# Part of the K phases on GpSimd, products by channel half, resident swapped spectra, and the last reads in two row groups

## The chip, the cores and the metric

One core of one Trainium2 chip. The metric is the device time of one execution in microseconds (us). "Time" below is a median over executions; the "span" of a profile runs from the first to the last instruction of the one execution that was profiled, and is about 2 us shorter than its time. Engine names are those of the profile: PE (TensorE), PEld (its weight loads), DVE (VectorE), ACT (ScalarE), POOL (GpSimd), SP (the queue that issues transfers). All runs compared here are in the fast state; single slower executions were left out by the comparison itself.

## The reference

One layer that mixes a long convolution with a gated feed-forward network, over 2048 tokens of 640 channels:

```python
g = sigmoid((x * gate_w).sum(-1, keepdims=True))
a = irfft(rfft(pad(u)) * rfft(pad(K)))[:L] + u * Dskip   # K[d,l] = Re sum_n C*dB*exp(dt*A*l)
b = (gelu(x @ w_gate) * (x @ w_up)) @ w_down
out = g * a + (1 - g) * b                                # x = u
```

## The kernel before

The kernel is one list of steps (some 900), each with a function and the buffers it reads and writes. A constant, `ORDER`, fixes the order of emission and the engine and PSUM bank of each step. So every change of the algorithm comes with a new order of all engines.

The kernel K of the convolution is made in two channel halves. For each half, "phases" (integer angles) are computed, ACT takes their sine, DVE combines the tables, and PE contracts them. These are the phases, all on DVE before:

```python
def phases(q, grid, i0):
    ...
    def go():
        for j in range(4):
            i, o = i0 + j, ph[:, 1, :, 4 * j:4 * j + 4]                  # 128x320
            if grid == 1:
                nc.vector.tensor_scalar(out=o, in0=quads(bK[:, ds]), scalar1=float(4 + 8 * i), ..., op0=ALU.mult)
            else:
                nc.vector.scalar_tensor_tensor(out=o, in0=quads(bK[:, ds]), ..., in1=quads(phiK[:, ds]), ...)
        nc.vector.tensor_scalar(out=ph[:, 0], in0=ph[:, 1], scalar1=PH / 4, ..., op0=ALU.add)   # 128x1280
```

The transforms go through memory: dU and dKA (spectra half-way), dY (the result before the last transform). For each of eight chunks c, `mix` loads dKA, finishes the K spectrum, multiplies it on DVE with the spectrum U and with its copy Us whose row pairs are swapped, and transforms back:

```python
def mix(u, us, kb, bi, c, UK, keys, R):
    ks = stageB(loadB(dKA[:], keys, bi, c, R), t, tn, R)
    ve(..., tensor_tensor(out=U,  in0=U,  in1=t, op=ALU.mult))     # 128x2560
    ve(..., tensor_tensor(out=Us, in0=Us, in1=t, op=ALU.mult))
    ...                                # inverse on PE, copies to t, write of t to dY chunk c
def finish(keys, rings, R):            # rings: four buffers
    for g in range(8):
        dma(640, ... out=t, in_=dY[:, 4 * g:4 * g + 4, :] ...)     # needs all dY chunks
        ...                            # two products on PE, DVE adds into the output, two output writes
```

## Time and profile before

| what | value |
|---|---|
| time | 329.29 us median of 3 (326.54 to 329.34) |
| profiled execution | 327.61 us, span 325.8 us |
| first / second K contraction starts on PE | 100.4 / 182.3 us |
| last forward matmul of K / last inverse starts | 238.4 / 295.7 us |

The prediction shows the lines that carry its argument. Four more matter later. From the groups of instructions (line, engine, operation, output and inputs, count, then busy time, mean ns of one, idle time before it) come the two-input products on DVE, whose means are the yardstick for any disturbance. From the list of transfers (count, KB each, median us from issue to landing) comes the dY round trip.

```profile
L637 DVE TENSOR_TENSOR arena<-arena 128x2560 bf16<-128x2560 bf16 x10 | 14.7, 1482 | 0.0
L631 DVE TENSOR_TENSOR arena<-arena 128x1280 bf16<-128x1280 bf16 x10 | 7.9, 816 | 1.0 <-ACT arena L627 1.0
...
dY<-arena SPq DMA_DIRECT2D x8, 640.0 KB, 6.1
arena<-dY SPq DMA_DIRECT2D x8, 640.0 KB, 5.6
```

### The profile page before, as it was taken

The numbers are of one execution on the slowest core, as the hardware profiler recorded it, in microseconds if no ns is written. First come the engines' busy times: TensorE is split into PE (matmuls) and PEld (weight loads), VectorE is DVE, ScalarE is ACT, GpSimd is POOL, SyncE is SP. The second block draws the span as 40 slices with busy tenths as digits, with TensorE's granted clock in tenths as the row PEclk, the third lists the DMA queues.
The fourth block names the chain that finished last, engine by engine and source line by source line (L and its number), as shares of the span: only waits on it lengthen the run. The fifth ranks groups of instructions, "written<-read, shape, count | busy, mean of one in ns | idle before, by whom it ended". The sixth has DMA issues, their size and how long they took to land.

```text
span 325.8 us, 5490 instructions
## 1 busy us (share of the span) xinstructions
PE 266.1 (82%) x2112; PEld 146.7 (45%) x2126; DVE 246.3 (76%) x332; ACT 223.6 (69%) x307; POOL 5.3 (2%) x18
## 2 busy tenths in 40 slices
PE   0799999897796999979899987985998889993452
PEld 0254444443366677534344743432465456551220
DVE  4687999999999963799996977254363899982464
ACT  4998997699995599998989576525471386671000
POOL 3000000000000000000000000000110000000000
PEclk9989999999797999999999997999899799998555
DMA  6993344332321144433437659979366569934997
GB/s 171 394 331 104 121 140 125 100 103 81 125 76 42 62 123 130 143 123 120 141 100 240 188 192 291 341 163 260 115 204 221 181 240 330 344 141 163 368 353 245
DMA packets 47519, 60.57 MB, mean 186 GB/s; under 512 B 4419, under 2 KB 41862, under 8 KB 47494
## 3 DMA queue, kind: packets, MB, share of 16 engines
q1 hardware_dynamic: 47494, 60.23, 57.3%
q8 instruction: 16, 0.26, 0.3%
q14 instruction: 9, 0.07, 0.1%
HBM read 35.80 MB, written 19.17 MB: 169 GB/s over the span
## 4 chain that ended last, share of the span: by engine, by line
PE 36%; ACT 22%; DVE 18%; DMA 15%; issue 5%; SPq 3%; DVEq 0%; ACTq 0%
PE ps L548 13%; PE ps L520 8%; PE ps L500 7%; ACT arena L243 6%; ACT arena L589 5%; DVE arena L247 5%; DMA dKA<-arena 4%; ACT arena L599 4%; DMA arena<-dY 3%; DMA arena<-dU 3%; ACT arena L504 3%; DMA arena<-dKA 2%; DVE arena L859 2%; PE ps L650 2%; PE ps L807 2%
## 5 line engine op out<-in xcount | busy, mean ns | idle before, releaser
L243 ACT CAST arena<-ps 128x640 bf16<-128x640 f32 x111 | 70.6, 702 | 38.1 <-PE ps L807 15.7
L500 PE MATMUL ps<-arena 128*128 128x512 bf16 x276 | 66.5, 392 | 13.0 <-DMA arena<-in_u_T_dram 9.2
L247 DVE CAST arena<-ps 128x640 bf16<-128x640 f32 (+2 forms) x67 | 56.2, 881 | 20.1 <-PE ps L807 10.4
L520 PE MATMUL ps<-arena 128*128 128x512 bf16 x250 | 63.1, 401 | 4.2 <-DVE arena L524 1.9
L548 PE MATMUL ps<-arena 128*128 128x320 bf16 x448 | 65.0, 305 | 1.0 <-DVE arena L247 0.5
L548 PEld LDWEIGHTS <-arena 128*128 128x128 bf16 x448 | 44.5, 100 | 20.6 <-issue 2.1
L500 PEld LDWEIGHTS <-arena 128*128 128x128 bf16 x280 | 28.0, 100 | 47.9 <-issue 14.1
L520 PEld LDWEIGHTS <-arena 128*128 128x128 bf16 x260 | 26.5, 103 | 37.2 <-issue 9.3
L589 ACT ACTIVATE arena<-arena 128x2560 bf16<-128x2560 int16 x18 | 41.6, 2334 | 0.4 <-DVE arena L637 0.3
L524 DVE TENSOR_TENSOR arena<-ps,arena 128x1024 bf16<-128x1024 f32 x26 | 31.6, 1218 | 13.1 <-PE ps L520 12.9
L504 ACT ACTIVATE arena<-ps 128x1024 bf16<-128x1024 f32 (+1 forms) x28 | 27.7, 1023 | 9.4 <-PE ps L500 9.2
L807 PE MATMUL ps<-arena 64*64 64x320 bf16 x256 | 16.9, 325 | 9.0 <-DMA arena<-dKA 2.8
L599 ACT ACTIVATE arena<-arena 128x320 bf16<-128x320 f32 x64 | 23.3, 455 | 1.0 <-DVE arena L451 1.0
L854 PE MATMUL ps<-arena 128*64 128x320 bf16 x64 | 10.2, 474 | 14.5 <-DMA arena<-dY 14.5
L859 DVE SCALAR_TENSOR_TENSOR arena<-ps,g_f,arena 128x640 bf16<-128x640 f32 x16 | 13.0, 878 | 11.9 <-PE ps L854 11.9
L249 DVE TENSOR_SCALAR arena<-ps,omg 128x640 bf16<-128x640 f32 x10 | 8.8, 883 | 14.9 <-PE ps L548 14.9
L627 ACT ACTIVATE arena<-arena 128x320 bf16<-128x320 f32 x40 | 14.8, 455 | 5.9 <-PE ps L650 5.9
L582 DVE SCALAR_TENSOR_TENSOR arena<-arena 128x320 int32<-128x320 f32 x40 | 16.9, 483 | 0.8 <-ACT arena L589 0.7
L650 PE MATMUL ps<-arena 128*128 128x80 bf16 x320 | 13.5, 212 | 3.8 <-DVE arena L637 2.8
L807 PEld LDWEIGHTS <-arena 64*64 64x64 bf16 x256 | 8.2, 107 | 17.7 <-issue 9.7
L650 PEld LDWEIGHTS <-arena 128*128 128x128 bf16 x320 | 13.3, 107 | 4.6 <-DVE arena L637 3.5
L780 PE MATMUL ps<-arena 128*128 128x320 bf16 x64 | 12.1, 308 | 4.1 <-DMA arena<-dS 2.3
(93 smaller groups left out, 240.8 us busy)
## 6 DMA issues: line engine op xcount, KB each, us to landing
arena<-in_w_gu_dram SPq DMA_DIRECT2D x52, 160.0 KB, 2.2
dU<-arena SPq DMA_DIRECT2D x16, 320.0 KB, 2.3
arena<-dU SPq DMA_DIRECT2D x8, 640.0 KB, 4.7
dKA<-arena SPq DMA_DIRECT2D x16, 320.0 KB, 4.2
arena<-arena SPq DMA_DIRECT2D x16, 320.0 KB, 4.3
arena<-dKA SPq DMA_DIRECT2D x8, 640.0 KB, 6.0
dY<-arena SPq DMA_DIRECT2D x8, 640.0 KB, 6.1
arena<-dY SPq DMA_DIRECT2D x8, 640.0 KB, 5.6
```

Source lines behind the costliest of these rows:

```text
L243: nc.scalar.copy(out=dst, in_=src(b))
L247: nc.vector.tensor_copy(out=dst, in_=src(b))
L500: nc.tensor.matmul(ps[:, k + j, :], lhsT=Wg[w][:, kt, :], rhs=xT[2 * grp + j][:, kt, :], start=(kt == 0), stop=(kt == NKT - 1))
L504: add({"ACT": an(1024)}, lambda s: nc.scalar.activation(out=HTall[0:p, :, f, :], in_=ps[0:p, plan.bank(g):plan.bank(g) + 2, :], func=ACT.G ...
L520: nc.tensor.matmul(ps[:, k + j, :], lhsT=Wu[w][:, kt, :], rhs=xT[2 * grp + j][:, kt, :], start=(kt == 0), stop=(kt == NKT - 1))
L524: add({"DVE": v1(1024)}, lambda s: nc.vector.tensor_tensor(out=HTall[:, :, f, :], in0=ps[:, plan.bank(u):plan.bank(u) + 2, :], in1=HTall[: ...
L548: nc.tensor.matmul(ps[:, k + h, 0:W], lhsT=HTq[q][:, f, 128 * j:128 * j + 128], rhs=Wd[f][:, W * h:W * h + W], start=(f == 0), stop=(f == ...
L589: ac(an(8 * W), lambda: nc.scalar.activation(out=t[:], in_=ph.bitcast(I16)[:, :, :, 0:32:2], func=ACT.Sin, scale=SIN_SCALE), r=[f"ph{k}"], ...
L599: nc.scalar.activation(out=cs1[:, 1, :, 4 * s:4 * s + 4], in_=quads(aT[:, ds]), func=ACT.Exp, scale=float(sg * (4 + 8 * i)))
L650: nc.tensor.matmul(ps[:, k + i // g, 80 * (i % g):80 * (i % g) + 80], lhsT=cs1[:, x, k0 + i, :], rhs=cs2[:, x, k0 + i, :], start=(x == 0), ...
L807: nc.tensor.matmul(ps[64 * y:64 * y + 64, k + x, 0:W], lhsT=TB[64 * x:64 * x + 64, 0, :], rhs=t[64 * x:64 * x + 64, 2 * a + y, HV[h]], sta ...
L859: add({"DVE": v1(D)}, lambda s, p=p, ph=ph, z=z: nc.vector.scalar_tensor_tensor(out=z, in0=ps[:, plan.bank(p):plan.bank(p) + 2, 0:W], scal ...
```

## The change

Its intent: take work from DVE in the first two stages (GpSimd was idle), begin spectral products when half of the channels are there, take the swap transfers out of the late stage, and read a part of dY before all of it is written.

```diff
-        def go():
+        def ts(s, **kw):
+            (nc.gpsimd if s["eng"] == "POOL" else nc.vector).tensor_scalar(**kw)
+        def go(s):
...
-        ve(4 * (v2(W) if grid == 1 else v1(W)) + v2(4 * W), go, ...)
+        e1 = {"DVE": 4 * (v2(W) if grid == 1 else v1(W))}
+        if grid == 1:
+            e1["POOL"] = 4 * pn(W)
+        add(e1, go, ...)
+        add({"DVE": v2(4 * W), "POOL": pn(4 * W)}, lambda s: ts(s, out=ph[:, 0], in0=ph[:, 1], ... op0=ALU.add), ...)
...
-    dKA = dp.tile([128, 32, D], BF16, name="dKA")
+    dKA = [dp.tile([128, 32, W], BF16, name=f"dKA{h}") for h in range(2)]
...
-    def mix(u, us, kb, bi, c, UK, keys, R):
+    def product(h, u, us, kb, bi, c, UK, keys, R):        # one channel half: U, Us times t, 128x1280 each
+    def inverse(u, us, yb, c, UK, R):
...
-    Us = blocks(O_CS1 + 40960, 4, 5120, 4, "Vs")
+    Us = (... eight buffers: every swapped spectrum stays ...)
...
+        for q in range(2):
+            p0, p1 = (0, 16 * cut) if q == 0 else (16 * cut, 128)       # cut = 4: rows 0-63, 64-127
+            for g, (t, nm) in enumerate(tiles):
+                dma(..., out=t[p0:p1], in_=dY[p0:p1, 4 * g:4 * g + 4, :], r=[("dY", c) for c in range(p0 // 16, p1 // 16)])
...
-    finish(ys, blocks(O_CS1, 4, 5120, 4, "as"), P["F1"])
+    finish(blocks(O_CS1, 4, 5120, 4, "as") + blocks(O_CS1 + 40960, 4, 5120, 4, "at"), P["F1"], 4)
```

`ORDER` is replaced as a whole. In it GpSimd gets 14 phase steps: 16 multiplications of 128x320 and 10 additions of 128x1280.

## The prediction

> **What bounds the kernel now.** I read the page's busy table first, then the row of 40 slices, then the windows (one table by stage), then the chain that ended last in order of time, and last the timeline of the final stage.
>
> ```profile
> PE 266.1 (82%) x2112; PEld 146.7 (45%) x2126; DVE 246.3 (76%) x332; ACT 223.6 (69%) x307; POOL 5.3 (2%) x18
> PE   0799999897796999979899987985998889993452
> DVE  4687999999999963799996977254363899982464
> POOL 3000000000000000000000000000110000000000
> ```
>
> No engine is full over the whole run, but each stage has its own limit: DVE (with ACT) to about 100 us, PE after that, nobody after 297. POOL does nothing. The windows say it in numbers (columns: window, length, busy of PE, PEld, DVE, ACT, POOL, granted clock, DMA share, GB/s):
>
> ```profile
> 40.00:80.00 40.00, 37.05 (x174) 17.12 (x176) 38.85 (x45) 35.57 (x46) 0.00 (x0) 1.00 0.38 111
> 80.00:120.00 40.00, 34.05 (x333) 23.78 (x334) 37.59 (x53) 32.34 (x49) 0.00 (x0) 0.87 0.25 78
> 275.00:290.00 15.00, 13.61 (x190) 8.83 (x192) 14.51 (x14) 9.45 (x16) 0.00 (x0) 1.00 0.77 268
> 300.00:310.00 10.00, 4.42 (x30) 2.04 (x32) 4.46 (x6) 0.00 (x0) 0.00 (x0) 0.50 0.84 318
> ```
>
> The end of the chain shows the tail. Read it as: the last down projection (L548) and the last inverse transform, then a round trip through memory, then a DVE-paced finish that twice waits for a read.
>
> ```profile
> 290.55 3.98 PE ps L548 x28
> ...
> 297.05 3.20 DMA dY<-arena
> 300.30 0.35 issue
> 300.74 3.89 DMA arena<-dY
> 304.67 0.76 PE ps L854 x3
> 305.54 1.53 DVE arena L859 x2
> 307.13 4.85 DVE arena L859 x6
> 311.98 0.31 SPq L863
> 312.38 7.01 DMA arena<-dY
> 319.43 0.76 PE ps L854 x4
> ```
>
> In the timeline of that stage the first five tiles reach L854 every 1.58 us (304.67, 306.25, ...), the last three at 313.65, 317.04 and 319.43: their buffers are reused, so their reads were issued late, behind output writes. The group rows I price with:
>
> ```profile
> L859 DVE SCALAR_TENSOR_TENSOR arena<-ps,g_f,arena 128x640 bf16<-128x640 f32 x16 | 13.0, 878 | 11.9 <-PE ps L854 11.9
> L826 DVE TENSOR_TENSOR arena<-arena 128x2560 bf16<-128x2560 bf16 x8 | 11.8, 1484 | 0.4 <-ACT arena L243 0.4
> L584 DVE TENSOR_SCALAR arena<-arena 128x1280 int32<-128x1280 int32 x18 | 14.9, 827 | 0.6
> dU<-arena SPq DMA_DIRECT2D x16, 320.0 KB, 2.3
> arena<-arena SPq DMA_DIRECT2D x16, 320.0 KB, 4.3
> ```
>
> **What the Trainium skill says.** First, "SBUF — State Buffer", section "Who interferes with whom": GpSimd and VectorE share one pair of ports under an exclusive lock, held for a whole instruction; VectorE needs it for tensor_scalar in a two-port mode and for two SBUF inputs (there against a GpSimd instruction that reads SBUF), while an instruction that reads PSUM and at most one SBUF input does not contend. The kernel before has no GpSimd instruction that reads SBUF, so its trace can't tell. Second, "GPSIMD Engine Reference", section "Engine selection": elementwise work is about twice as slow there for two inputs, roughly line rate for one. The moved instructions have one input; the nearest thing in this trace is an iota of 128x1024 at 1046 ns, against 827 ns for L584's 128x1280 on DVE. Third, "SBUF — State Buffer", section "Door 1: The DMA port swizzle": partitions 0 to 63 reach only 8 of 16 ports. The trace agrees: 320 KB on 64 partitions took 4.3 us, 320 KB on 128 took 2.3 us. Fourth, "VectorE: DVE Perf Modes", on the TRN2 errata: a fixed cost per instruction, about 150 cycles. It agrees: a bf16 product of 128x1280 (L613) has a mean of 819 ns, one of 128x2560 1484 ns, so two halves cost 154 ns more.
>
> **The change part by part.**
>
> (1) GpSimd. In the built order GpSimd gets 4 of the 8 groups of four grid-1 phases (128x320) and 10 of the 18 adds of 128x1280. DVE sheds 16 x 0.26 + 10 x 0.83 = 12.4 us; 8 of the short instructions and 6 of the adds, 7.0 us, belong to the first K half. On GpSimd I estimate 0.5 and 1.4 us each from the iota's slope, so 16 x 0.5 + 10 x 1.4 = 22 us. By the lock, part of that comes back as DVE waiting; DVE reads PSUM in about a quarter of the stage to the first contraction (12 of L524 at 1.22 and 7 evacuations at 0.8: 20 of 85 us) and idles in some more, so at best half of the saving is kept.
>
> (2) Products by half. 16 products of 1.48 become 32 of 0.82: 26.2 instead of 23.7, so DVE pays 2.5 us. In return half 0 (its reads of the K spectrum, 64 of the L807 matmuls, half the products) no longer waits for half 1. The writes of the K spectrum also get rows of 1280 instead of 640 bytes.
>
> (3) Resident swapped spectra. Eight swap transfers (320 KB, 4.3 us each) leave the stage after 245 us, where the DMA share is 0.77, for the stage before. No engine's work changes.
>
> (4) Last reads in two row groups, eight separate buffers: rows 0 to 63 are read while the last chunks are computed; after the last dY write only 8 x 320 KB are left, all issued at once. They reach half the ports, so I keep 1.58 us a tile and no bandwidth gain; the gain is that tiles six to eight no longer arrive late: 1.1 + 1.7 + 0.7 = 3.5 us of DVE waiting from the timeline. The floor of the finish is 16 x 0.84 = 13.4 us on DVE.
>
> (5) A new order on every engine. This is the largest part. I priced the built order of PE with the durations before (ten matmuls of L500 or L520 2.16, 28 of L548 3.95, four of L719 0.55, of L780 0.72, of L807 0.33, 24 of L650 1.03, 16 of L834 0.72). PE work ahead of four points: the first K contraction, the second, the last K forward matmul (L780), the last inverse (L834).
> Before: 73.5, 149.6, 197.3, 250.7 us. They happened at 100.4, 182.3, 238.5 and 296.0.
> After: 63.9, 137.7, 200.2, 246.8 us.
>
> Stage 1, to the first contraction. PE does not pace it. Summing the durations before over the built orders, ACT has 89.9 us up to its last needed Sin, as before (90.1, reached at 98.1). DVE has 85.2 instead of 92.9, plus GpSimd's lock. ACT starts about half a microsecond sooner (its parameters are the first transfers) and loses its 2.5 us wait for the reciprocal, which now comes early. I put the contraction at 98, 2.4 earlier. PE gets there with 9.6 us less work done, which is a debt.
> Stage 2, to the second contraction: PE 73.8, DVE 69, ACT 71 (before 76.2, 72, 74 in 81.9). All three are as tight as before, so I scale: 79.4 us, so 177.5.
> Stage 3, to the last L780: PE 62.5 instead of 47.7. The extra work is filler where PE waited before: 56.2 us elapsed for 47.7. I expect 4 us of idle, 66.5, so 244.
> Stage 4, to the last L834: PE 46.6 instead of 53.4, because less of the transforms is left and one down projection (3.95) now comes after it. Before, 57.5 us elapsed, 4 above the sum; I take 50, so 294.
> Tail: evacuation, dY write and read 8.65 (296.0 to 304.67), first matmuls 0.87, DVE 13.4, last output 3.9 (321.9 to 325.8): 26.8. Span about 321. The moved down projection fits into the 8.65.
>
> The sum is a span 5 us shorter (1.5%). The ledger: tail 3, down projection 4, filler in stage 3 some 4 to 5, contraction 2.4, against 9.6 us of debt and a little DVE.
>
> **The rivals.** (a) GpSimd gives more than I kept: the lock is mostly taken beside PSUM work and stage 1 ends at 95; then stage 2 is looser too and the span is 312 to 316. For it: DVE at 97% of 40 to 80. Against: ACT is at 89% and has the same sum. (b) GpSimd's lock turns against DVE: each 1.4 us add stalls a DVE that would have needed 0.83; stage 1 ends at 103, and the time is 327 to 331. For it: three quarters of DVE's work in stage 1 reads and writes SBUF alone. (c) DMA becomes the bound: the swaps pile up with the gathers of half 1 (windows 200 to 215 already show a share of 0.96), and the early row-group reads sit ahead of the last dY writes, which also have only two buffers. That would cost 3 to 8 us and eat the tail's gain. Against: dY chunks come 5.4 us apart on PE (1.44 + 3.95), slow enough for the queue to drain.
>
> **Range and chances.** The stage sum gives 321 of span. Times run 1.8 (the profiled run, 327.61) to 3.5 us (the median) above it: 324. A new order that prepares filler work for each known wait is more often underrated than overrated by such a sum, since I scaled each stage by the old inefficiency; so I move the centre to 320, 2.8% under 329.3. Rivals b and c make the upper edge 328, rival a the lower 311. The 2% line is 322.7, close to the centre: faster 0.62, within 0.34, slower 0.04.
>
> **What would show it.** Right: the first contraction at 95 to 100; PE idle of at most 5 us between the second contraction and the last L780; L854's matmuls every 1.7 us without gaps and under 28 us from the last inverse to the end; the last L548 inside the dY round trip; GpSimd busy about 22 us. Wrong: the mean of DVE's SBUF products above 819 and 1484 ns beside GpSimd (rival b); late landings of dY writes or of K gathers (rival c); a first contraction before 94 (rival a).

## The result, and the profile after

The kernel after takes 343.69 us (median of four, 338.89 to 344.64; the slowest counts as slow and is left out of the ratio, a fifth execution of 341.48 is in it), the kernel before 329.06 us over the same rounds. Ratio 1.0409, 95% interval 1.031 to 1.0509: slower. A ratio here is the mean time of the one kernel's fast runs over that of the other's fast runs of the same rounds, so not quite the ratio of the medians. The profiled execution took 338.89 us (span 337.1); it is the fastest of them, so the table below understates the loss a little.

The same four points, and the end, as predicted and as seen:

| stage ends with | before | predicted | after | duration predicted | duration after |
|---|---|---|---|---|---|
| first K contraction starts | 100.4 | 98 | 106.7 | 98 | 106.7 |
| second K contraction starts | 182.3 | 177.5 | 183.5 | 79.4 | 76.8 |
| last forward matmul of K | 238.4 | 244 | 254.7 | 66.5 | 71.2 |
| last inverse starts | 295.7 | 294 | 304.3 | 50 | 49.6 |
| end of span | 325.8 | 320.8 | 337.1 | 26.8 | 32.8 |

The miss is in three stages: 8.7 us in the first, 4.7 in the third, 6.0 in the last; the second gives 2.6 back.

Next come the page's busy line and the slices of DVE and POOL. The sum of work that the order gives DVE has gone down, but its busy time has gone up by 15 us, and POOL's phase steps take 56.1 us where 22 were estimated (two lines below):

```profile
PE 266.6 (79%) x2110; PEld 145.0 (43%) x2126; DVE 261.0 (77%) x327; ACT 223.9 (66%) x304; POOL 61.4 (18%) x44
...
DVE  4978999999999979999887914433997799732564
...
POOL 4900640534675404040000000000001100000000
```

Below are the groups of POOL and of DVE, different shapes kept apart. POOL's addition takes 3.56 us and its multiplication 1.28 in the mean; on DVE, in the run without GpSimd phases, the same steps take 0.82 (mean) and 0.25 (busy time by count). POOL's means include time in which it was itself held beside DVE: its shortest addition took 3.44 us, its shortest multiplication 1.01. The DVE products of 128x1280 and 128x2560 of the K chain have means of 1020 and 1776 ns where they had 816 and 1482, and DVE's own additions 1240 where they had 827:

```profile
L582 POOL TENSOR_SCALAR arena<-arena 128x1280 int32<-128x1280 int32 x10 | 35.6, 3557 | 59.5 <-DVE arena L590 41.9 <-DVE arena L582 16.5 <-ACT arena L638 0.9
L582 POOL TENSOR_SCALAR arena<-arena 128x320 int32<-128x320 f32 x16 | 20.5, 1283 | 29.8 <-ACT arena L600 24.9 <-DVE arena L458 4.1
```

```profile
L648 DVE TENSOR_TENSOR arena<-arena 128x2560 bf16<-128x2560 bf16 x10 | 17.7, 1776 | 1.4 <-ACT arena L600 1.4
...
L642 DVE TENSOR_TENSOR arena<-arena 128x1280 bf16<-128x1280 bf16 x10 | 10.0, 1020 | 0.0
L582 DVE TENSOR_SCALAR arena<-arena 128x1280 int32<-128x1280 int32 x8 | 9.9, 1240 | 0.3
```

The timeline shows how. First DVE from 60 to 71 us, then POOL in the same time (start, length):

```profile
60.30 6.10 DVE L590 SCALAR_TENSOR_TENSOR arena<-arena 128x320 int32<-128x320 f32 x8
66.32 0.81 DVE L642 TENSOR_TENSOR arena<-arena 128x1280 bf16<-128x1280 bf16 x1
67.06 0.81 DVE L252 CAST arena<-ps 128x640 bf16<-128x640 f32 x1
67.79 2.87 DVE L642 TENSOR_TENSOR arena<-arena 128x1280 bf16<-128x1280 bf16 x1
70.59 0.81 DVE L252 CAST arena<-ps 128x640 bf16<-128x640 f32 x1
```

```profile
62.08 3.62 POOL L582 TENSOR_SCALAR arena<-arena 128x1280 int32<-128x1280 int32 x1 [15.95 <-DVE arena L590]
66.56 3.88 POOL L582 TENSOR_SCALAR arena<-arena 128x1280 int32<-128x1280 int32 x1 [0.85 <-ACT arena L638]
```

Read the second addition: it ends at 66.56 + 3.88 = 70.44. The copy from PSUM that starts inside it (67.06) takes its usual 0.81 us. The product that follows (67.79), two inputs in SBUF, ends at 70.66, just after POOL is done. The eight instructions at 60.30 take 6.10 us around the first addition; in the run without GpSimd phases (a1 below) they take 3.31. Even an instruction of 32 columns took 3.42 us at 14.08 (0.30 in a1), until POOL's run that began at 8.00 ended 9.46 us later. The kernel after, then a1:

```profile
14.08 3.42 DVE L406 TENSOR_SCALAR arena<-arena,sc 128x32 int32<-128x32 int32 x1
8.00 9.46 POOL L582 TENSOR_SCALAR arena<-arena 128x320 int32<-128x320 f32 x5 [4.10 <-DVE arena L458]
```

```profile
58.16 3.31 DVE L591 SCALAR_TENSOR_TENSOR arena<-arena 128x320 int32<-128x320 f32 x8
14.44 0.30 DVE L407 TENSOR_SCALAR arena<-arena,sc 128x32 int32<-128x32 int32 x1
```

Taken one by one in the trace, seven DVE instructions of the kernel after took 1.8 to 3.2 us longer than the shortest of their kind, 17.7 us together, each beside one of the ten additions. No DVE instruction that reads PSUM was stretched by more than 0.1 us.

The last stage has a second trouble. In the queue's timeline, seven reads of rows 0 to 63 (L861) are issued before the sixth of the eight dY writes (L854, at 295.58). That write takes 10.75 us to land, where the slowest recorded one of the kernel before took 7.6. The results on their way to dY have two buffers, and ACT waits 7.1 us for one; in the kernel before no engine waited for a dY write from 270 us on:

```profile
291.15 4.31 SPq L861 DMA_DIRECT2D arena<-dY  x7
295.58 0.52 SPq L854 DMA_DIRECT2D dY<-arena  x1
...
300.16 8.27 SPq L854 DMA_DIRECT2D dY<-arena  x2
```

```profile
ACT arena L248 <- DMA dY<-arena: 7.1, 1, 7.1
```

### The profile page after: what moved, and what is told of

It is laid out like the page before. It is cut to its first block, busy times and chain, and to the rows that moved or that the text cites. A ratio compares the mean times of both kernels' runs of the same rounds, so it can differ in the third digit from the quotient of the medians.

```text
span 337.1 us, 5542 instructions
## 1 busy us (share of the span) xinstructions
PE 266.6 (79%) x2110; PEld 145.0 (43%) x2126; DVE 261.0 (77%) x327; ACT 223.9 (66%) x304; POOL 61.4 (18%) x44
## 3 DMA queue, kind: packets, MB, share of 16 engines
q1 hardware_dynamic: 45702, 60.23, 59.2%
## 4 chain that ended last, share of the span: by engine, by line
DVE 31%; PE 21%; ACT 19%; DMA 16%; issue 7%; SPq 4%; POOLq 0%; DVEq 0%; ACTq 0%
PE ps L525 7%; PE ps L505 6%; ACT arena L248 5%; ACT arena L600 4%; DMA dY<-arena 4%; DVE arena L252 4%; PE ps L553 4%; DVE arena L529 3%; DMA arena<-dY 3%; DVE arena L590 3%; DVE arena L648 3%; ACT arena L509 3%; DVE arena L624 2%; ACT arena L610 2%; DVE arena L465 2%
## 5 line engine op out<-in xcount | busy, mean ns | idle before, releaser
L505 PE MATMUL ps<-arena 128*128 128x512 bf16 x271 | 69.8, 409 | 21.4 <-DMA arena<-in_w_gu_dram 14.5
L525 PE MATMUL ps<-arena 128*128 128x512 bf16 x253 | 65.1, 405 | 12.4 <-ACT arena L509 4.5
L252 DVE CAST arena<-ps 128x640 bf16<-128x640 f32 (+2 forms) x71 | 59.8, 876 | 16.4 <-PE ps L817 10.9
L582 POOL TENSOR_SCALAR arena<-arena 128x320 int32<-128x320 f32 (+1 forms) x26 | 56.1, 2158 | 89.3 <-DVE arena L590 41.9
L553 PE MATMUL ps<-arena 128*128 128x320 bf16 x448 | 64.7, 304 | 2.7 <-ACT arena L248 2.6
L505 PEld LDWEIGHTS <-arena 128*128 128x128 bf16 x280 | 28.8, 104 | 59.1 <-issue 17.8
L553 PEld LDWEIGHTS <-arena 128*128 128x128 bf16 x448 | 44.0, 99 | 22.1 <-issue 4.2
L525 PEld LDWEIGHTS <-arena 128*128 128x128 bf16 x260 | 26.2, 102 | 46.3 <-issue 19.9
L610 ACT ACTIVATE arena<-arena 128x320 bf16<-128x320 f32 x64 | 23.4, 454 | 1.5 <-DVE arena L456 1.5
L590 DVE SCALAR_TENSOR_TENSOR arena<-arena 128x320 int32<-128x320 f32 x40 | 22.6, 626 | 1.7 <-ACT arena L600 1.7
L897 POOL IOTA arena<- 128x1024 int32 x2 | 2.1, 1044 | 116.3 <-DMA dKA<-arena 104.4
L648 DVE TENSOR_TENSOR arena<-arena 128x2560 bf16<-128x2560 bf16 x10 | 17.7, 1776 | 1.4 <-ACT arena L600 1.4
L582 DVE TENSOR_SCALAR arena<-arena 128x320 int32<-128x320 f32 (+1 forms) x24 | 14.5, 648 | 2.3 <-ACT arena L600 2.0
```

The source lines that it names most:

```text
L252: nc.vector.tensor_copy(out=dst, in_=src(b))
L505: nc.tensor.matmul(ps[:, k + j, :], lhsT=Wg[w][:, kt, :], rhs=xT[2 * grp + j][:, kt, :], start=(kt == 0), stop=(kt == NKT - 1))
L525: nc.tensor.matmul(ps[:, k + j, :], lhsT=Wu[w][:, kt, :], rhs=xT[2 * grp + j][:, kt, :], start=(kt == 0), stop=(kt == NKT - 1))
L553: nc.tensor.matmul(ps[:, k + h, 0:W], lhsT=HTq[q][:, f, 128 * j:128 * j + 128], rhs=Wd[f][:, W * h:W * h + W], start=(f == 0), stop=(f == ...
L582: (nc.gpsimd if s["eng"] == "POOL" else nc.vector).tensor_scalar(**kw)
L610: nc.scalar.activation(out=cs1[:, 1, :, 4 * s:4 * s + 4], in_=quads(aT[:, ds]), func=ACT.Exp, scale=float(sg * (4 + 8 * i)))
```

## The experiments

Theory at the start: GpSimd's operations are far slower than estimated and hold DVE up (first stage), and the early reads delay the dY writes (last stage). Rival: the new order, with its late first matmul (14.5 us against 7.45) or its halves, costs it. Each chip has its own level, so runs of different rows are compared by their ratio to the kernel before.

| run | what it is | time | ratio to before, 95% interval |
|---|---|---|---|
| a1_no_gpsimd | after, phases back on DVE | 330.55 | 1.0060 (1.0033 to 1.0087) |
| a2_whole_reads | after, whole late reads | 341.09 | 1.0395 (1.0365 to 1.0426) |
| a3_both | both edits | 328.42 | 0.9995 (0.9964 to 1.0025) |
| b1_gpsimd_alone | before, 14 phase steps on GpSimd | 337.49 | 1.0295 (1.0257 to 1.0332) |
| b2_eight_reads | before, 8 read buffers | 326.07 | 0.9895 (0.9839 to 0.9951) |
| b3_down_last | before, last projection moved | 325.85 | 0.9880 (0.9797 to 0.9962) |
| b4_both_tail | before, b2 and b3 | 324.73 | 0.9933 (0.9907 to 0.9959) |
| c1_weights_first | a3, other first transfers | 328.02 | 0.9983 (0.9953 to 1.0014) |
| d1_reads_in_order | a3, two reads exchanged | 326.62 | 1.0010 (0.9976 to 1.0044) |
| d2_early_tokens | d1, TensorE's first inputs first | 329.41 | 1.0073 (1.0047 to 1.0100) |
| e1_idle_gpsimd | a1 with idle GpSimd work (spoilt) | 342.00 | 1.0452 (1.0369 to 1.0534) |
| e2_idle_long | a1 with idle GpSimd work | 356.74 | 1.0862 (1.0804 to 1.0919) |
| g1_short_only | after, only the multiplications on GpSimd | 335.17 | 1.0235 (1.0170 to 1.0299) |
| g2_long_only | after, only the additions on GpSimd | 340.50 | 1.0382 (1.0319 to 1.0445) |
| f1_gpsimd_fp32 | after, GpSimd in fp32 | 341.63 (one run) | state unknown |

All give the right result except f1, which is wrong on purpose.

### Taking the two suspects away

a1 changes 14 entries of the order from POOL to DVE, at the same places. a2 replaces the two row groups by one whole read per tile:

```diff
-        for q in range(2):
-            p0, p1 = (0, 16 * cut) if q == 0 else (16 * cut, 128)
...
+        for g, (t, nm) in enumerate(tiles):
+            dma(640, ... out=t, in_=dY[:, 4 * g:4 * g + 4, :], r=[("dY", c) for c in range(8)], w=[nm])
```

> The kernel after, with its fourteen phase steps (16 multiplications of 128x320, 10 additions of 128x1280) put back from GpSimd on VectorE, at the same places in the order. Theory (slow GpSimd work holds VectorE up): the first K contraction comes back from 106.7 to 98-101 us, no 3 us copies of 32 columns are left on VectorE, time 333-337 against 343.7 of the kernel after. Rival (the new order of the first stage, above all the later first matmul at 14.5 us, costs it): first contraction stays above 104, time 341-346, as VectorE then has some 12 us more of its own work.

> The kernel after, with the eight last reads whole (128 partitions each), issued after the last write of dY, all ahead of the outputs as before. Theory (the early reads of row group 0 lie ahead of the last dY writes and hold the two dY buffers): the dY write issued at 295.6 lands in 3-5 us instead of 10.75, VectorE and ScalarE lose their waits of 2.4 and 7.0 us for it, and the time falls by 3-5 us to 339-341. Rival (the reads are not what the tail waits for): within 1.5 us of 343.7; or slower by up to 3, if the early halves did save reading time.

> Both edits at once: no GpSimd phases and whole late reads. What is left of the change: products by halves, resident swaps, eight read buffers, the new order. Theory: the two losses add, 328-332, about the kernel before (329.1). Rival (order, halves or the pile of transfers in the third stage cost the rest): 334-340.

Measured: a1 gives back 3.5% (1.0409 to 1.0060), more than was expected; a2 almost nothing by itself, but on top of a1 the same edit gives 0.65% (1.0060 to 0.9995). a2's mechanism was as expected: ACT's and DVE's waits for dY writes (7.1 and 2.4 us) are gone (the sixth write's landing is missing from a2's trace, so the 3 to 5 us expected for it stay unchecked). From the last inverse to the end it takes 30.7 us instead of 32.8. That this hardly shows in its time is within the scatter of the kernel after, whose fast runs differ among themselves by 1.4%.

| point | predicted | a1 | a3 |
|---|---|---|---|
| first contraction | 98 | 98.3 | 98.1 |
| second contraction | 177.5 | 173.4 | 173.7 |
| last forward matmul of K | 244 | 244.6 | 244.3 |
| last inverse | 294 | 294.6 | 295.7 |
| end | 320.8 | 327.1 | 325.8 |

Without GpSimd four of the five points come out within 4.1 us of the prediction, three of them within 2 us in both runs. A part of that is luck: in a1 the second stage took 75.1 us where 79.4 were predicted, and the third 71.2 where it was 66.5, so that two errors of over 4 us cancel at 244.6. What stays is the end: 32.5 us from the last inverse in a1, 30.1 in a3, against 26.8 predicted.

### GpSimd alone, in the old order

b1 splits the phase step of the kernel before in two, as the change does, and gives GpSimd the same number of steps:

```diff
-    ve(4 * (...) + v2(4 * W), go, ...)                  # one step on VectorE
+    add(e1, go, ...); add({"DVE": ..., "POOL": ...}, lambda s: ts(s, out=ph[:, 0], ...))
 ORDER: each phase step becomes two at the same place; 4 and 10 of them on GpSimd
```

> The kernel before, with the same number of phase steps of the same groups on GpSimd (16 multiplications of 128x320 and 10 additions of 128x1280), nothing else changed. Theory: a multiplication takes 1.28 us and an addition 3.4-3.6 us there, VectorE's instructions beside them stretch, and the time rises by 5-12 us to 334-341. Rival (GpSimd work is harmless by itself, only the new order makes it costly): 326-331.

Measured: 1.0295, so GpSimd costs some 9 us without anything else of the change (in the change itself it is 3.5%, by a1). DVE's busy time is 255.9 us where it was 246.3 (9.6 more), the span 335.0 where it was 325.8 (9.2 more). The rival is out: the new order is not needed for this loss.

### Held port or late results

GpSimd can cost time in two ways: DVE is stretched beside it, or something waits for its results. In e1 and e2 DVE does all phases and GpSimd does work that nobody reads; g1 and g2 split the change's own GpSimd work by length. e1 has idle multiplications of 128x320, three of them for each addition. The edit of e2 (of a1; the multiplications likewise):

```diff
+        def idle2(s):
+            if s["i"] in GP:                       # the steps that GpSimd had
+                nc.gpsimd.tensor_scalar(out=scr2, in0=ph[:, 1], scalar1=PH / 4, ..., op0=ALU.add)
```

> The kernel without GpSimd phases (VectorE does all of them), and beside it GpSimd does idle copies of the same kind, about as long in all as its phases took (16 and 30 multiplications of 128x320 into a scrap buffer), whose results nobody reads. Theory (GpSimd's turns on the shared port stretch VectorE's instructions): the time rises from 330.6 to 338-345, though nothing waits for GpSimd, and VectorE's busy time from 250.7 to 262-275. Rival (what costs is only the waiting for GpSimd's results): 330-332, VectorE's busy time under 254.

e1 rose by 3.9% over a1, but it is spoilt: the scrap buffer lay where the contraction's results go, and copies on ACT and DVE waited 6.1 and 4.7 us for GpSimd there. Only its first 102.6 us (a1: 98.3) are free of that. One number of it still counts: DVE's busy time rose by 6.2 us to 256.9, between the two expectations, although its 46 short multiplications kept GpSimd busy for 64.1 us. It was repeated with a scrap buffer that the first contraction does not touch:

> The kernel after with all phases on VectorE, and beside it idle GpSimd work of the same shapes and number as its phases had (16 multiplications of 128x320, 10 additions of 128x1280, here with a bf16 result) into a scrap buffer that nothing needs before the first contraction is done. Theory (the shared port): VectorE's busy time rises from 250.7 by 15-24 us, time 338-346 against 330.6. Rival (late results): nothing waits for them here, so 330-332.

g1 and g2 are the kernel after with a part of its 14 entries set back:

```diff
 ORDER, g1: the 10 additions from GpSimd to VectorE
 ORDER, g2: the 4 steps of four multiplications from GpSimd to VectorE
```

> The kernel after with only the 16 multiplications of 128x320 on GpSimd (20 us of its time), the 10 additions back on VectorE. If the sum of GpSimd's time decides: a third of the loss of 3.5%, so 333-335. If the length of one operation decides (a VectorE instruction waits at most 1.28 us here): under 1% over the kernel without GpSimd phases, 329-333; VectorE's busy time 248-254.

> The kernel after with only the 10 additions of 128x1280 on GpSimd (36 us of its time), the multiplications back on VectorE. If the sum of GpSimd's time decides: two thirds of the loss, 337-339. If the length of one operation decides: nearly all of it, 339-343; VectorE's busy time 256-262.

Measured in e2: 1.0862. Nothing needs GpSimd's results (no engine waits for them in the trace), and the time rises by 8.0% over a1, more than was expected. DVE's busy time rises from 250.7 to 277.0, 26.3 us, and the span by 28.5. Of these, 25.8 us are lost by the second contraction (199.2 against 173.4), so in the stages in which GpSimd works; the lower granted clock of that execution (0.893 against 0.950) can account for little of it, as the stages after that differ by 2.7 us. The busy line of e2 and three of its groups (a1 has 485 and 821 ns for the two on DVE):

```profile
PE 274.5 (77%) x2110; PEld 148.8 (42%) x2126; DVE 277.0 (78%) x353; ACT 224.0 (63%) x304; POOL 64.5 (18%) x44
```

```profile
L592 POOL TENSOR_SCALAR arena<-arena 128x1280 bf16<-128x1280 int32 x10 | 35.5, 3551 | 71.4 <-DVE arena L604 52.9 <-DVE arena L588 18.1
```

```profile
L604 DVE SCALAR_TENSOR_TENSOR arena<-arena 128x320 int32<-128x320 f32 x40 | 25.2, 693 | 1.0 <-ACT arena L616 0.9
L588 DVE TENSOR_SCALAR arena<-arena 128x1280 int32<-128x1280 int32 x18 | 22.5, 1261 | 0.2
```

So GpSimd's work beside DVE suffices, without any late result. That a held port does it fits what the timeline shows of SBUF and PSUM instructions; no run tests the port by itself. The stretch also closes the account of the change: DVE sheds 16 x 0.25 + 10 x 0.82 = 12.2 us of work, yet its busy time is 10.3 us above a1's (261.0 against 250.7), so some 22.5 us are stretch (21.4 when added up instruction by instruction, 19.2 of them beside additions); and the span is 10.0 us above a1's.

g1 and g2: the long additions alone cost 1.0382 / 1.0060, 3.2%, nearly all of the loss, with DVE at 261.7 us busy (11.0 above a1) and the span 11.0 above, as the "length" theory expected. The short ones alone cost 1.7%. That is more than the "length" theory allowed (under 1%) and agrees better with the "sum" theory (333 to 335), but the trace shows a third way: DVE is hardly stretched there (248.6 us, 2.1 below a1 for 4.0 us of work less) and instead waits for GpSimd's results, since its own addition follows each group of multiplications. The profiled execution of g1 is its slowest (338.23 us; the median is 335.17), so what it shows may be more than the usual. This is DVE's wait in g1, up to 200 us (total, times, longest):

```profile
DVE arena L583 <- POOL arena L583: 8.3, 4, 2.5
```

So both ways exist: the long operations stretch, the short ones came late. In the change itself the additions follow on GpSimd too, and DVE waits for none of them (ACT once, for 1.0 us); this may be why the two losses alone, 3.2 and 1.7%, sum to more than the 3.5% of both. Per us of GpSimd's time the stretch on DVE was 0.40 in the kernel after (22.5 of 56.1), 0.44 in e2 (26.3 of 59.2), and with short multiplications alone 0.10 in e1 (6.2 of 64.1).

### Is it the integer conversion?

f1 gives GpSimd's steps fp32 on both sides:

```diff
+            if s["eng"] == "POOL":
+                kw = dict(kw, out=kw["out"].bitcast(FP32))
+                if kw["op0"] == ALU.add:
+                    kw["in0"] = bK[:, 0:80, None].to_broadcast([128, 80, 16])
```

> The kernel after, with GpSimd's phase steps in fp32 on both sides instead of int32 out (a wrong result on purpose). If the integer conversion makes GpSimd slow: an addition of 128x1280 falls from 3.44 us to 1.2-1.7 us, a multiplication of 128x320 from 1.28 to 0.4-0.6 us. If it is GpSimd's rate for any such operation: both stay within 15% of what they were.

```profile
L587 POOL TENSOR_SCALAR arena<-arena 128x1280 f32<-128x1280 f32 x10 | 36.6, 3666 | 49.6 <-ACT arena L605 49.3
L587 POOL TENSOR_SCALAR arena<-arena 128x320 f32<-128x320 f32 x16 | 20.4, 1278 | 39.4 <-ACT arena L605 34.6 <-DVE arena L459 3.9
```

The means are 3.67 and 1.28 us, and the shortest single ones 3.44 and 1.01 us, as with integers. So it is not the conversion: GpSimd is as slow for this operation with either type.

### The end: eight buffers, the moved projection, the order of the reads

b2 gives the kernel before the eight read buffers and moves all reads ahead of the outputs in the order; b3 moves two entries of the order; b4 does both.

```diff
-    finish(ys, blocks(O_CS1, 4, 5120, 4, "as"), P["F1"])
+    finish(ys, blocks(O_CS1, 4, 5120, 4, "as") + blocks(O_CS1 + 40960, 4, 5120, 4, "at"), P["F1"])
 ORDER, b2: the eight reads of dY directly behind the last write of dY
 ORDER, b3: the last projection group and its copy behind the last inverse (PSUM pair 1)
```

> The kernel before, with eight buffers for the last reads instead of four and all eight whole reads issued ahead of the outputs. Prediction's step 4 (VectorE's 3.5 us of waiting for reads in the end part come free): 325-326. Rival, seen in the end part of the run with both edits (last read landed 3.5 us earlier, at 315.9 instead of 319.4, and yet the last product ended at 321.8 as before): the reads and outputs share one stream of transfers that is full, so what the reads gain the outputs lose: 327.5-329.5.

> The kernel before, with its last projection group (28 matmuls, 3.98 us at 290.55 in the chain of waits, and its copy) moved behind the last inverse on TensorE, into the round trip of dY. Prediction's step: the last inverse and all after it come 3-4 us earlier, 324.5-326. Rival (the products on VectorE, not TensorE, release the last inverse, or the tail is full anyway): 327.5-329.5.

> The kernel before with eight read buffers, all reads ahead of the outputs, and its last projection group behind the last inverse: the two edits that gave 1.05% and 1.2% by themselves. If they add: ratio 0.976-0.980, 320.5-322.5. If they share the same wait: 0.985-0.99, 324-326.

Measured: each gave about 1%, as the prediction's steps said; but together they gave 0.67% (20 runs), not 2%. b3 shows where the moved projection goes: the last inverse starts at 292.9 instead of 295.7, and no more, because DVE's products are then next. The chain of waits of b3 (start, length), where before there stood 3.98 us of projection at 290.55, is:

```profile
289.12 1.49 DVE arena L826
290.62 1.41 DVE arena L827
292.03 0.04 issue
292.07 0.63 PE ps L834 x12
```

In b4 the same two products stand there, and in its profiled execution the last inverse starts at 295.3, only 0.4 us earlier than before; but this execution (326.95 us) is the slowest of b4's twenty.

b2 shows what eight buffers are worth. Its finish on DVE has no gap:

```profile
304.84 12.99 DVE L859 SCALAR_TENSOR_TENSOR arena<-ps,g_f,arena 128x640 bf16<-128x640 f32 x16 [8.52 <-PE ps L854]
```

It ends at 317.8 instead of 321.9, but the span ends at 324.2: the output writes that had gone out between the reads now stand behind them. From the last inverse to the end it is 29.1 us in b2 and 30.1 in the kernel before. So of the 3.5 us of waiting that the buffers remove (3.3 by DVE's gaps in the timeline), 1.0 reaches the end. That the two together do not give 2% is measured. How much of either 1% is real is not: b2 and b3 have four runs each, and their intervals reach down to 0.5 and 0.4%. Gains as small as these would add to 0.9%, which is inside b4's interval, so it is not shown that they fail to add.

In a3 both edits are present and nothing is gained. One reason is in the order itself: the reads are issued for tiles 4, 3, 6, 5, 7, 2, 1, 0, but five of the sixteen products, the two of tile 0 among them, wait for that last read. d1 exchanges the last two reads in the order (4, 3, 6, 5, 7, 2, 0, 1). This is a3's finish on DVE, in three stretches with gaps, the last of 4.05 us after the last read landed at 315.9:

```profile
305.33 4.12 DVE L873 SCALAR_TENSOR_TENSOR arena<-ps,g_f,arena 128x640 bf16<-128x640 f32 x5 [4.41 <-PE ps L868]
310.81 4.84 DVE L873 SCALAR_TENSOR_TENSOR arena<-ps,g_f,arena 128x640 bf16<-128x640 f32 x6 [1.35 <-PE ps L868]
317.75 4.05 DVE L873 SCALAR_TENSOR_TENSOR arena<-ps,g_f,arena 128x640 bf16<-128x640 f32 x5 [2.10 <-PE ps L868]
```

> The kernel with both edits (no GpSimd phases, whole late reads), with the last two of its eight reads exchanged, so that the reads come in the order in which the products use them: there the seventh and eighth read are used by products 15, 16 and 12, 13, and five products waited for the last read. Theory (this hides what the eight buffers gain): the last product ends 2.5 us after the last read instead of 5.9, time 325-326.5 against 328.4. Rival (the outputs behind it fill the stream of transfers anyway): 327.5-329.5.

Measured: the last product ends at 318.8 instead of 321.8, and the end comes 29.0 us after the last inverse instead of 30.1, but the ratio is 1.0010 (0.9976 to 1.0044): no gain that the runs can tell. As in b2, the output writes end last.

### The early row groups

The pair a1 and a3 measures them: 0.65%, and 32.5 against 30.1 us at the end. The windows show what the reads did (window, length, busy of PE, PEld, DVE, ACT, POOL, granted clock, DMA share, GB/s). First comes a3, where whole tiles are read, then a1 with its row groups:

```profile
310.00:316.00 6.00, 3.21 (x24) 1.40 (x22) 4.84 (x6) 0.00 (x0) 0.00 (x0) 0.50 1.02 410
```

```profile
310.00:316.00 6.00, 3.65 (x26) 1.62 (x24) 4.67 (x6) 0.00 (x0) 0.00 (x0) 0.50 1.02 203
```

The transfers are busy all the time in both (a share of 1.02, so the share does not show the loss), but on half the partitions they move 203 GB/s instead of 410. So the row groups halve the bytes that are left after the last dY write, at half of the rate: from the issue of the first of these reads to the landing of the last it is 15.0 us in a1 (302.15 to 317.2) and 15.5 in a3 (300.37 to 315.9). Next to nothing is gained, and the delayed dY write is the price.

### The late first matmul

c1 and d2 put TensorE's first inputs ahead of parameters:

```diff
 ORDER, first transfers (c1: of a3, d2: of d1; P parameters, w gate or up weights, x0 to x3 token tiles)
-  P P P P P P x2 x1 x0 w w P
+  c1: P P P P P P w x2 w x1 x0 P
+  d2: w P P x0 P P P P x1 w x2 P
```

> The kernel with both edits (no GpSimd phases, whole late reads), with the first transfers in another order: the first gate weights (160 KB) and one token tile ahead of the last parameters and of the other token tiles, so that TensorE need not wait for 14.2 us. Theory (TensorE bounds all four stages, so its late start is carried to the end): first matmul at 8-10 us, time 323.5-326 against 328.4. Rival (the K chain on VectorE and ScalarE sets the first stage, TensorE has slack in it): first matmul early, but 327.5-329.5.

> The kernel before this one in this list, with the gate weights and the token tile that TensorE needs first really ahead of the last parameters (the earlier try moved a tile that is used later, and the first matmul came at 13.9 us). Theory (TensorE's late start is carried to the end): first matmul at 7-9 us, 2-4 us faster than the kernel without the earlier start, 321.5-324. Rival (the K chain sets the first stage): within 1 us of it.

c1 moved the wrong token tile: the first matmul still came at 13.9 us, so its 0.9983 tells nothing. d2 moved the right one. Its first matmul comes at 7.62 us, as intended, but DVE waits 4.2 us for parameters, the first contraction starts at 100.6 instead of 97.8, and the kernel is slower (1.0073 against 1.0010). TensorE's start some 6.5 us earlier shows as a gain in no stage (the first contraction at 100.6 us, then 75.1, 70.8, 51.6 and 28.9 against d1's 75.6, 69.8, 51.5 and 29.0). This agrees with the rival: the K chain sets the first stage, and TensorE has slack in it. An earlier start that costs DVE nothing was not tried, so that the late first matmul costs nothing is not shown.

## Why the prediction was wrong

It said 320 us, with a range of 311 to 328; it was 343.69. By its own steps:

- **(1) GpSimd: the step that failed.** It put 0.5 and 1.4 us on the two operations, "16 x 0.5 + 10 x 1.4 = 22 us", from the slope of an iota and from the Trainium skill's "roughly line rate". They took 1.28 and 3.56 us, 56.1 us in all (at the least 1.01 and 3.44 each). An iota reads nothing, so its slope was no price for an instruction that reads SBUF; and no run had such a price. From the wrong length followed the wrong balance: "at best half of the saving is kept" became the whole saving lost and 10.3 us more on top. The lock itself was named, with the right test (DVE's SBUF products above 819 and 1484 ns), and that test came out as rival (b): 1020 and 1776. Rival (b) had the first contraction at 103; it was 106.7. It too reckoned with 1.4 us an addition.
- **(2) Products by half.** The 128x1280 products on DVE have means of 819 and 820 ns, as priced. The writes of the K spectrum got rows of 2560 bytes in the code, not 1280, and land no sooner (4.5 us, before 4.2). Not tested alone.
- **(3) Resident swaps.** Not tested alone. They came into the third stage beside the K gathers, as rival (c)'s first half has it: that stage took 71.2 us instead of 66.5, and as long without GpSimd (a1: 71.2). PE was busy for 60.5 of them (a1: 60.6) and idle for 10.7, where 4 were predicted and 5 were the limit under "Right". But the waits of PE that a1's profile names there end with ACT for 7.4 us and with a transfer for 2.1, so that a pile of transfers is the cause is not shown; it was not tried.
- **(4) Last reads.** "1.58 us a tile and no bandwidth gain" was right: as the Trainium skill has it ("SBUF — State Buffer", section "Door 1: The DMA port swizzle"), 64 partitions of one half reach half of the ports, and here they moved 203 GB/s against 410. What the prediction took for a sign of this in the trace before was none: the 320 KB that took 4.3 us are swaps from SBUF to SBUF between every second partition of all 128, not transfers on partitions 0 to 63. "3.5 us of DVE waiting" was right as waiting and wrong as gain: b2 shows that the outputs move behind the reads and 1.0 us is left. The counter-argument against rival (c), "slow enough for the queue to drain", failed: a dY write issued behind seven row-group reads kept ACT waiting for 7.1 us. Of the 6 us missed at the end, the row groups account for 2.4 (a1 against a3); the rest is mostly the gain that was counted and never came (a3 takes 30.1 us there, as the kernel before).
- **(5) The new order.** Without GpSimd the stage points came at 98.3, 173.4, 244.6 and 294.6, and all but the second were right in number. But the first was predicted with GpSimd's help, and a1 reaches it without: the help was not needed. And the third and fourth are right because a second stage 4.3 us shorter and a third stage 4.7 us longer than predicted cancel, which is luck. The moved projection was counted with 3.95 us; in the old order it made the last inverse 2.8 us earlier (b3) and then met DVE's products.
- **Centre and chances.** Moving the centre down because a new order "is more often underrated" had no number behind it. The sums of the rivals (b) and (c) were on paper at 327 to 331 plus 3 to 8 us, and the range stopped at 328: the two were treated as alternatives, and (b) and a part of (c) both happened. Even their sum, 330 to 339, stops short of 343.69.

What stays open: a3, with all that the change has beyond GpSimd and the row groups, is no faster than the kernel before, although it contains the two edits that give b4 its 0.67%. So, if the two edits are worth as much there, halves, resident swaps and the new order together lose about that much, and no run separates them. The best version that is well measured is b4 (twenty runs), 0.9933 of the kernel before and faster than both; b2 and b3 have lower ratios from four runs each, with intervals that overlap b4's.

## What to carry to other kernels

An idle engine is not free help: where two engines share a port, price the helper's instruction from a trace of that very instruction before moving work to it, and count a part of its length once more as stretch on the other engine (here 0.4 of it with long additions in the mix, 0.1 with short multiplications alone). A wait that is removed in front of a full stream of transfers moves behind it; ask what stands last in the stream. And when two rivals do not exclude each other, add them before setting the edge of the range.

## What the Trainium skill lacked or had wrong

- "GPSIMD Engine Reference", section "Engine selection", calls one-input elementwise work roughly line rate on GpSimd. Here a one-input tensor_scalar of 128x1280 took 3.56 us on GpSimd (3.67 in fp32; at the least 3.44 in both) against 0.82 on VectorE, and one of 128x320 took 1.28 (at the least 1.01) against 0.25.
- "SBUF — State Buffer", section "Who interferes with whom", is right about who waits: products with two SBUF inputs and tensor_scalar were held (2.87 instead of 0.82 us, 3.42 instead of 0.30), copies from PSUM were not (0.81). It gives no size for a whole kernel: here 59 us of idle GpSimd work (e2) stretched VectorE by 26 us and the span by 28.5.
